# Attention decode with a mixer MLP: the last K transpose moved up in a block, and the wo products laid out as two wide rows

## Chip, core and metric

The program runs on one core of a Trainium2 chip. Its time is the device time of one execution in microseconds; the median of several executions is compared.

## The reference

One token, x of width 1024, goes through two branches whose results are added to x. What is computed, cut to what matters:

```python
xn = layernorm(x)
# A: attention over a cache of 65,536 positions, 4 KV heads of 8 query heads each, 128 wide
q = (xn @ wq).reshape(32 heads, 128)
p = softmax(q . k_cache * 128 ** -0.5)        # k_cache, v_cache: [4, 65536, 128] bf16
o = p . v_cache
A = o.reshape(4096) @ wo                      # wo: [4096, 1024]
# B: a mixer and an MLP on the same xn
h  = gelu(layernorm(xn) @ w1); hs = shift(h) @ w2; x1 = xn + hs
B  = x1 + gelu(layernorm(x1) @ w3) @ w4       # w4: [3584, 1024]
out = x + A + B
```

With one position the shifts of the mixer leave nothing of h, so the product with w2 is taken with a vector of zeros. The two caches are 64 MB each; with the weights some 170 MB are read.

## The kernel before, in words

The program is raw engine code. Python helpers record each operation in the list of its engine (`_Q`), with the semaphore waits that its buffers (`_B`) call for, and the lists are emitted in that order: what stands earlier in the source is earlier on its engine. DMAs are issued by SP, in order, each after the waits of its own buffers, so a DMA that waits holds up those behind it.

SBUF has three slots of 64 KB per partition, KV[0] to KV[2]. The weights wq, w1, w2 and w3 use them first (lines 295 to 451: the query and the MLP's hidden vector gh_bf). Then the caches stream through in NBLK = 8 blocks of 32,768 positions, two for each KV head: K of a block takes slot 0 or 2 in turn, V always slot 1. Behind the last V, wo goes into slot 0, and w4 into slot 2 in four pieces of 17, 7, 3 and 1 rows (`w4_parts`).

A block has four sub-tiles n to n+3, and a softmax for each half, 2m and 2m+1. The functions that the loop at line 585 calls:

- `Ttr(n)` (L460), on DVE: transposes a sub-tile of K in place, as 32-bit words.
- `QK(n)` (L474), on TensorE: 16 products of 512 columns, four side by side in four column groups, into PSUM bank n % 4 of `S_ps`.
- `MAX(g)` (L481 to 484): the row maxima of two banks on DVE, and a small product that spreads them.
- `EXP(g)` (L491 to 502): the running bound on DVE, the exponential of two banks on ACT into `p_sb`.
- `PT(n)` (L505) and `PTr(n)` (L509): the probabilities turned by a product into the one bank `PT_ps`, and from there by a DVE transpose into half n % 2 of `pT_f`.
- `PV(n)` (L518): 16 products with V into `OT_ps`.
- `FLUSH(g)` (L529, L531): adds the half's result to `O_acc` on DVE.
- `combine(h)` (L535 to 550): at the end of a head, the normalised output into `o_bf`.
- `issue(i)`: the load of V of the next block, and then of K of the block after it. V's waits for the last PV of this block, since V has one slot.

TensorE's instructions of a head are one loop body, run four times; the other engines' are written out.

After the loop, `out_resid` and `out_rows` make the sum of x, xn, the mixer's part, wo and w4 in bank 0 of `S_ps`, as four rows of 256 columns at partitions 0, 32, 64 and 96. A product there has one column of weights and 256 moving columns. A last DVE copy (L637) and one DMA bring it out.

Of the kernel before, what the change touches and what calls it, by code (L numbers as in the profile page):

```python
# [8 lines left out]
ACTF = mybir.ActivationFunctionType  # L9
# [107 lines left out]
def _op(q, fn, reads=(), writes=(), partial=False, loop=False):  # L117
    _deps(q, reads, writes)
    ev = q.op(fn, True, loop)
    _done(ev, reads, writes, partial)  # L120
    return ev


def _grp(q, fns, reads=(), writes=(), partial=False):
    _deps(q, reads, writes)
    ev = None
    for i, fn in enumerate(fns):
        ev = q.op(fn, i == len(fns) - 1)
    _done(ev, reads, writes, partial)
    return ev  # L130
# [16 lines left out]
def bass_parallel_sum__gqa_block_cached__mixer_s_mlp__decode_kernel(  # L147
# [14 lines left out]
    D = A_x.shape[2]  # L162
# [5 lines left out]
    KT_D = D // P  # L168
# [10 lines left out]
    with ExitStack() as es:  # L179
# [195 lines left out]
        fns = []  # L375
# [80 lines left out]
        def Ttr(n):  # L456
            m, sub = divmod(n, 4)
            s = slot(3 + 2 * m)
            o = 4096 * sub
            _op(q_dve, lambda e: e.transpose(out=KV32[:, s, o:o + 4096], in_=KV32[:, s, o:o + 4096]), reads=[b_KV[s][sub]], writes=[b_KV[s][sub]], loop=True)  # L460
# [5 lines left out]
        def QK(n):  # L466
            m, sub = divmod(n, 4)
            s = slot(3 + 2 * m)
            fns = []
            for we in range(4):  # L470
                w_hi, e_ = divmod(we, 2)
                for cm in range(4):
                    mv = bass.AP(KV[:].tensor, s * SLOT + sub * 8192 + cm * 128 + w_hi * 64 + e_, [[kvstep, P], [512, 16], [2, 32]])
                    fns.append(lambda e, we=we, cm=cm, mv=mv: e.matmul(  # L474
                        S_ps[32 * cm:32 * cm + 32, n % 4, :], Ycur[:, we, :, :].rearrange("p a g -> p (a g)"), mv,
                        start=(we == 0), stop=(we == 3), tile_position=(0, 32 * cm)))
            _grp(q_pe, fns, reads=[b_KV[s][sub], b_Yc], writes=[b_S[n % 4]])

        def MAX(g):
            k = g % 2  # L480
            _op(q_dve, lambda e: e.reduce_max(mrow[:, k:k + 1], S_ps[:, 2 * k:2 * k + 2, :].rearrange("p b c -> p (b c)"), axis=AX.X), reads=b_S[2 * k:2 * k + 2], writes=[b_mrow[k]])  # L481
            _op(q_dve, lambda e: e.tensor_tensor(out=Rm[:, k, :], in0=sel16[:, :], in1=mrow[:, k:k + 1].broadcast_to([P, 16]), op=ALU.mult),  # L482
                reads=[b_mrow[k], b_const], writes=[b_R[k]], loop=True)
            _op(q_pe, lambda e: e.matmul(M_ps[:, 0:16], Lmat[:, :], Rm[:, k, :], start=True, stop=True),  # L484
                reads=[b_R[k], b_const], writes=[b_M])

        def EXP(g):
            k, o = g % 2, 1 - g % 2
            first = g % (2 * BPH) == 0
            if first:  # L490
                _op(q_dve, lambda e: e.tensor_reduce(out=brun[:, k:k + 1], in_=M_ps[:, 0:16], axis=AX.X, op=ALU.min), reads=[b_M], writes=[b_brun[k]])  # L491
            else:
                _op(q_dve, lambda e: e.tensor_reduce(out=Bst[:, k:k + 1], in_=M_ps[:, 0:16], axis=AX.X, op=ALU.min), reads=[b_M], writes=[b_B[k]])
                _op(q_dve, lambda e: e.tensor_tensor(out=brun[:, k:k + 1], in0=brun[:, o:o + 1], in1=Bst[:, k:k + 1], op=ALU.min),  # L494
                    reads=[b_brun[o], b_B[k]], writes=[b_brun[k]])
            _op(q_act, lambda e: e.activation(p_sb[:, :, :].rearrange("p b c -> p (b c)"), S_ps[:, 2 * k:2 * k + 2, :].rearrange("p b c -> p (b c)"), ACTF.Exp,  # L496
                                              bias=brun[:, k:k + 1], scale=SCALE, accum_out=lp[:, k:k + 1]),
                reads=b_S[2 * k:2 * k + 2] + [b_brun[k]], writes=b_p + [b_lp[k]], loop=True)
            if not first:
                _op(q_dve, lambda e: e.tensor_tensor(out=dd[:, k:k + 1], in0=brun[:, k:k + 1], in1=brun[:, o:o + 1], op=ALU.subtract),  # L500
                    reads=[b_brun[o], b_brun[k]], writes=[b_dd[k]])
                _op(q_act, lambda e: e.activation(ff[:, k:k + 1], dd[:, k:k + 1], ACTF.Exp), reads=[b_dd[k]], writes=[b_ff[k]])

        def PT(n):
            _op(q_pe, lambda e: e.matmul(PT_ps[:, :], permR[:, :], p_sb[:, n % 2, :], start=True, stop=True),  # L505
                reads=[b_p[n % 2], b_const], writes=[b_PT])

        def PTr(n):
            _op(q_dve, lambda e: e.transpose(out=pT_f[:, n % 2, :], in_=PT_ps[:, :]), reads=[b_PT], writes=[b_pT[n % 2]], loop=True)  # L509

        def PV(n):
            m, sub = divmod(n, 4)
            s = slot(4 + 2 * m)
            g, last = divmod(n, 2)
            fns = []
            for q in range(16):
                q4 = q % 4
                fns.append(lambda e, q=q, q4=q4: e.matmul(OT_ps[32 * q4:32 * q4 + 32, g % 2, :], pT_bf[:, n % 2, q, :, 1],  # L518
                                                          KV[:, s, 8192 * sub + 512 * q:8192 * sub + 512 * (q + 1)],
                                                          start=(last == 0 and q < 4), stop=(last == 1 and q >= 12), tile_position=(0, 32 * q4)))  # L520
            _grp(q_pe, fns, reads=[b_pT[n % 2], b_KV[s][sub]], writes=[b_OT[g % 2]], partial=(last == 1))
# [40 lines left out]
        def out_rows(items, reads, last=False):  # L562
            fns = []
            for lhs, rhs in items:
                for jj in range(4):
                    fns.append(lambda e, lhs=lhs, rhs=rhs, jj=jj: e.matmul(  # L566
                        S_ps[32 * jj:32 * jj + 1, 0, 0:256], lhs, rhs[:, 256 * jj:256 * jj + 256],
                        start=False, stop=last, tile_position=(0, 32 * jj), skip_group_check=True))
            _grp(q_pe, fns, reads=reads, writes=[b_OUT], partial=True)

        def out_resid():
            fns = []
            for j in range(KT_D):
                for jj in range(4):
                    fns.append(lambda e, j=j, jj=jj: e.matmul(
                        S_ps[32 * jj:32 * jj + 1, 0, j:256:8], acc[:, j:j + 1], ident_f[:, 32 * jj:32 * jj + 32],
                        start=(j == 0), stop=False, tile_position=(0, 32 * jj), skip_group_check=True))
            _grp(q_pe, fns, reads=[b_acc, b_const], writes=[b_OUT])

        def loop_sync(h):  # L580
            if h > 0:
# [3 lines left out]
        for m in range(NBLK):  # L585
            n = 4 * m
            h, nb = divmod(m, BPH)
            if nb == 0:
                loop_sync(h)
                q_pe.mark({q.loop_sem: q.count[q.loop_sem] for q in (q_dve, q_act)})  # L590
                YC(h)
            Ttr(n)
            QK(n)
            Ttr(n + 1)
            QK(n + 1)
            Ttr(n + 2)
            MAX(2 * m)
            EXP(2 * m)
            QK(n + 2)
            PT(n)  # L600
            PTr(n)
            PT(n + 1)
            PTr(n + 1)
            Ttr(n + 3)
            PV(n)
            QK(n + 3)
            if m == NBLK - 1:
                for i in range(len(w4_parts)):
                    for bk in b_KV[2]:
                        for sv, vv in list(bk.r.items()) + list(bk.w.items()):  # L610
                            b_W4[i].add_read((sv, vv))
                    w4_dma(i)
            PV(n + 1)
            MAX(2 * m + 1)
            EXP(2 * m + 1)
            FLUSH(2 * m)
            PT(n + 2)
            PTr(n + 2)
            PT(n + 3)
            PTr(n + 3)  # L620
            PV(n + 2)
            PV(n + 3)
            FLUSH(2 * m + 1)
            issue(6 + 2 * m)
            if m == NBLK - 2:
                kv_load(0, "wo", A_wo.rearrange("(p r) n -> p (r n)", p=P), SLOT)
            else:
                issue(7 + 2 * m)
            if nb == BPH - 1:
                combine(h)  # L630
        loop_sync(HKV)
        q_pe.mark({q.loop_sem: q.count[q.loop_sem] for q in (q_dve, q_act)})
        out_resid()
        out_rows([(o_bf[:, j:j + 1], KV[:, 0, j * D:(j + 1) * D]) for j in range(32)], b_KV[0] + [b_o])
        for i, (r0, nr) in enumerate(w4_parts):
            out_rows([(gh_bf[:, r:r + 1], KV[:, 2, r * D:(r + 1) * D]) for r in range(r0, r0 + nr)], [b_W4[i], b_gh], last=(i == len(w4_parts) - 1))
        _op(q_dve, lambda e: e.tensor_copy(orow[:, :], OUT), reads=[b_OUT], writes=[b_orow])  # L637
# [82 lines left out]
```

## Time and profile before

| | us |
|---|---|
| median of 9 executions | 403.44 (401.97 to 405.21) |
| the profiled execution, time | 402.67 |
| its span, first to last instruction | 401.3 |
| busy: DVE, PE, ACT, POOL | 223.0, 183.4, 23.3, 7.1 |
| the 16 DMA engines' share of the span, queue q1 | 98.5% |
| mean granted TensorE clock | 0.608 |

The span is what the profile covers; the time of the same execution is 1.37 us more. In the views, L12 is line 12 of the kernel; PE is a TensorE product and PEld the load of its weights; a wait is given with the instruction that ended it. The chain of waits is followed back from the last instruction. Timeline lines give start and length in us. A line of the table of windows gives a stretch of the span, its length, the busy time of PE, PEld, DVE, ACT and POOL with the number of instructions, the granted TensorE clock, the busy share of the DMA engines and what they moved in GB/s. The share can exceed 1 a little in a short stretch, as a packet is counted where it begins.

### The profile page before, as it was taken

To read this page: it belongs to the slowest core of one execution; us is meant where nothing else is said; L and a number is where in the kernel's file an instruction comes from. 1 tells how busy PE (TensorE), PEld (TensorE's weight loads), DVE (VectorE), ACT (ScalarE), POOL (GpSimd) and SP (SyncE) were. 2 spreads that over 40 slices of the span, in tenths; PEclk is the share of its full clock that TensorE was granted. 3 is DMA by queue.
4 is the path that set the end of the run, shared out by engine and by line. 5 is a ranking of instruction groups with operands and counts; after the bars stand their busy time and mean duration, and the time that the engine had idled before them with its cause. 6 is when DMAs were issued, how large, how long until landed. Compare 5 with 4: busy or idle time off the path is not lost.

```text
span 401.3 us, 3672 instructions
## 1 busy us (share of the span) xinstructions
PE 183.4 (46%) x1627; PEld 65.9 (16%) x1627; DVE 223.0 (56%) x259; ACT 23.3 (6%) x49; POOL 7.1 (2%) x30
## 2 busy tenths in 40 slices
PE   0044767254335553561357235614551464245625
PEld 0022435011101120120012101101120111001323
DVE  0024221966397549645964795467748772976300
ACT  1000000011001100110011000101010101011000
POOL 5000000000000000000000000000000000000000
PEclk9997666556655555566557655555585555555776
DMA  9999999999999999999999999999999999999995
GB/s 418 418 394 482 394 491 425 420 418 431 400 431 425 470 400 438 431 444 405 438 425 425 425 444 451 438 419 431 431 418 444 438 438 438 425 418 425 418 416 208
DMA packets 3760, 169.99 MB, mean 424 GB/s; under 512 B 548, under 2 KB 552, under 8 KB 808
## 3 DMA queue, kind: packets, MB, share of 16 engines
q1 hardware_dynamic: 3608, 169.87, 98.5%
q8 instruction: 6, 0.10, 0.1%
q10 hardware_dynamic: 144, 0.00, 0.0%
q14 instruction: 2, 0.02, 0.0%
HBM read 169.87 MB, written 0.00 MB: 423 GB/s over the span
## 4 chain that ended last, share of the span: by engine, by line
DMA 55%; DVE 25%; PE 17%; issue 1%; ACT 1%; SPq 1%; POOL 0%
DMA KV<-in_A_k_cache_dram 42%; DVE KV L460 17%; DMA KV<-in_B_w_dram 8%; DMA KV<-in_A_x_dram 5%; PE S_ps L474 4%; PE OT_ps L518 3%; PE S_ps L411 3%; DVE pT_f L509 2%; PE M_ps L426 2%; PE PT_ps L505 2%; PE S_ps L379 1%; DVE mrow L481 1%; ACT p_sb L496 1%; DVE Yall L395 1%; DVE pT_f L419 1%
## 5 line engine op out<-in xcount | busy, mean ns | idle before, releaser
L460 DVE STREAM_TRANSPOSE KV<-KV 128x4096 f32<-128x4096 f32 x32 | 140.0, 4412 | 14.5 <-DMA KV<-in_A_k_cache_dram 14.5
L474 PE MATMUL S_ps<-KV,Ycur 128*32 128x512 bf16 x512 | 60.7, 623 | 97.5 <-DVE KV L460 97.5
L518 PE MATMUL OT_ps<-KV,pT_f 128*32 128x512 bf16 x512 | 57.4, 613 | 7.2 <-DMA KV<-in_A_v_cache_dram 7.2
L509 DVE STREAM_TRANSPOSE pT_f<-PT_ps 128x512 f32<-128x512 f32 x32 | 23.0, 717 | 34.1 <-PE PT_ps L505 34.1
L474 PEld LDWEIGHTS S_ps<-KV,Ycur 128*32 128x32 bf16 x512 | 14.3, 126 | 133.9 <-DVE KV L460 116.3
L496 ACT ACTIVATE p_sb<-S_ps,brun 128x1024 bf16<-128x1024 f32 x16 | 17.8, 1114 | 280.4 <-DVE brun L494 189.8
L505 PE MATMUL PT_ps<-p_sb,permR 128*128 128x512 bf16 x32 | 18.1, 567 | 26.6 <-ACT p_sb L496 13.6
L481 DVE TENSOR_REDUCE mrow<-S_ps 128x1 f32<-128x1024 f32 x16 | 19.3, 1205 | 16.0 <-PE S_ps L474 16.0
L518 PEld LDWEIGHTS OT_ps<-KV,pT_f 128*32 128x32 bf16 x512 | 17.4, 137 | 39.4 <-issue 27.4
L529 DVE SCALAR_TENSOR_TENSOR O_acc<-O_acc,ff,OT_ps 128x512 f32<-128x512 f32 x12 | 8.9, 745 | 21.9 <-PE OT_ps L518 21.9
L484 PE MATMUL M_ps<-Rm,Lmat 128*128 128x16 bf16 x16 | 3.1, 193 | 30.3 <-DVE Rm L482 30.2
L411 PE MATMUL S_ps<-KV 128*32 128x512 bf16 x88 | 12.6, 565 | 2.7 <-DVE KV L359 2.7
L339 DVE CAST KV<-KV 128x8 f32<-128x8 bf16 x1 | 0.2, 172 | 22.1 <-DMA KV<-in_A_x_dram 22.1
L637 DVE CAST orow<-S_ps 128x256 bf16<-128x256 f32 x1 | 0.4, 425 | 18.8 <-PE S_ps L566 18.8
L505 PEld LDWEIGHTS PT_ps<-p_sb,permR 128*128 128x128 bf16 x32 | 3.3, 102 | 41.2 <-ACT p_sb L496 21.0
L566 PE MATMUL S_ps<-KV,gh_bf 128*1 128x256 bf16 x112 | 6.0, 381 | 8.9 <-DMA KV<-in_B_w_dram 8.9
L426 PE MATMUL M_ps<-ident_f,pT_f 64*128 64x2 f32 (+2 forms) x32 | 7.9, 373 | 2.4 <-DVE pT_f L419 2.4
L484 PEld LDWEIGHTS M_ps<-Rm,Lmat 128*128 128x128 bf16 x16 | 1.6, 103 | 43.8 <-DVE Rm L482 43.8
L426 PEld LDWEIGHTS M_ps<-ident_f,pT_f 64*128 64x128 f32 (+2 forms) x32 | 7.7, 326 | 4.7 <-DVE pT_f L419 3.3
L419 DVE COPY pT_f<-S_ps 64x512 f32<-64x512 f32 (+1 forms) x3 | 2.1, 686 | 11.3 <-PE S_ps L411 11.3
L364 PE MATMUL M_ps<-KV 8*128 8x8 bf16 x1 | 0.2, 184 | 15.9 <-DVE Dmat_f L363 15.9
L379 PE MATMUL S_ps<-KV 128*32 128x512 bf16 x64 | 6.0, 556 | 1.4 <-DVE KV L359 1.4
(83 smaller groups left out, 86.8 us busy)
## 6 DMA issues: line engine op xcount, KB each, us to landing
KV<-in_B_w_dram SPq DMA_DIRECT2D x1, 7168.0 KB, 48.0
KV<-in_B_w_dram SPq DMA_DIRECT2D x1, 4352.0 KB, 24.7
KV<-in_B_w_dram SPq DMA_DIRECT2D x2, 2048.0 KB, 28.1
KV<-in_B_w_dram SPq DMA_DIRECT2D x1, 1792.0 KB, 28.6
KV<-in_B_w_dram SPq DMA_DIRECT2D x1, 768.0 KB, 30.0
KV<-in_B_w_dram SPq DMA_DIRECT2D x1, 256.0 KB, 30.2
KV<-in_A_k_cache_dram SPq DMA_DIRECT2D x8, 42.9
KV<-in_A_v_cache_dram SPq DMA_DIRECT2D x8, 24.0
```

Source lines behind the costliest of these rows:

```text
L379: fns.append(lambda e, j=j, b=b, jj=jj: e.matmul(S_ps[32 * jj:32 * jj + 32, b, :], xn_bf[:, j:j + 1].broadcast_to([P, 32]), KV[:, 0, j * H ...
L411: fns.append(lambda e, j=j, k=k, mv=mv: e.matmul(S_ps[32 * (k % 4):32 * (k % 4) + 32, bank + k // 4, :], vec[:, j:j + 1].broadcast_to([P, ...
L419: _op(q_dve, lambda e, b=b, nb=nb: e.tensor_copy(pT_f[0:32 * nb, b, :], S_ps[0:32 * nb, bank + b, :]), reads=[b_S[bank + b]], writes=[b_pT ...
L426: fns.append(lambda e, b=b, nb=nb, c=c: e.matmul(M_ps[:, c0 + 16 * b + c:c0 + 16 * b + 4 * nb:4], pT_f[0:32 * nb, b, c:512:4], ident_f[0:3 ...
L460: _op(q_dve, lambda e: e.transpose(out=KV32[:, s, o:o + 4096], in_=KV32[:, s, o:o + 4096]), reads=[b_KV[s][sub]], writes=[b_KV[s][sub]], l ...
L474: fns.append(lambda e, we=we, cm=cm, mv=mv: e.matmul(S_ps[32 * cm:32 * cm + 32, n % 4, :], Ycur[:, we, :, :].rearrange("p a g -> p (a g)") ...
L481: _op(q_dve, lambda e: e.reduce_max(mrow[:, k:k + 1], S_ps[:, 2 * k:2 * k + 2, :].rearrange("p b c -> p (b c)"), axis=AX.X), reads=b_S[2 * ...
L496: _op(q_act, lambda e: e.activation(p_sb[:, :, :].rearrange("p b c -> p (b c)"), S_ps[:, 2 * k:2 * k + 2, :].rearrange("p b c -> p (b c)") ...
L505: _op(q_pe, lambda e: e.matmul(PT_ps[:, :], permR[:, :], p_sb[:, n % 2, :], start=True, stop=True), reads=[b_p[n % 2], b_const], writes=[b ...
L509: _op(q_dve, lambda e: e.transpose(out=pT_f[:, n % 2, :], in_=PT_ps[:, :]), reads=[b_PT], writes=[b_pT[n % 2]], loop=True)
L518: fns.append(lambda e, q=q, q4=q4: e.matmul(OT_ps[32 * q4:32 * q4 + 32, g % 2, :], pT_bf[:, n % 2, q, :, 1], KV[:, s, 8192 * sub + 512 * q ...
L529: _op(q_dve, lambda e: e.scalar_tensor_tensor(out=O_acc[:, 0:512], in0=O_acc[:, 0:512], scalar=ff[:, k:k + 1], in1=OT_ps[:, k, :], op0=ALU ...
```

## The change

In the loop, `Ttr(n + 3)` comes right after the first half's `EXP`, ahead of `PT(n)`; `QK(n + 3)` follows `PTr(n)`. The second half's `MAX` and `EXP` come before `PV(n)`, and `PV(n)`, `PV(n + 1)` and `FLUSH(2m)` are woven among the second half's `PT`. In the last block the w4 loads stand behind `QK(n + 3)`, as before.

In the tail, the residual and wo are summed in bank 1 as two rows of 512 columns at partitions 0 and 32: 16 products in place of 32, and 64 in place of 128. One row is then copied by DVE, the other by ACT, into half 0 of `pT_f`, whose first 64 partitions POOL has set to zero; four fp32 products with columns of the identity carry the quarters of the two rows to the four rows of bank 0, on which the w4 products add as before.

```diff
--- before.py
+++ after.py
@@ -568,14 +568,23 @@
                         start=False, stop=last, tile_position=(0, 32 * jj), skip_group_check=True))
             _grp(q_pe, fns, reads=reads, writes=[b_OUT], partial=True)
 
-        def out_resid():
-            fns = []
-            for j in range(KT_D):
-                for jj in range(4):
-                    fns.append(lambda e, j=j, jj=jj: e.matmul(
-                        S_ps[32 * jj:32 * jj + 1, 0, j:256:8], acc[:, j:j + 1], ident_f[:, 32 * jj:32 * jj + 32],
-                        start=(j == 0), stop=False, tile_position=(0, 32 * jj), skip_group_check=True))
-            _grp(q_pe, fns, reads=[b_acc, b_const], writes=[b_OUT])
+        def resid_rows():
+            _grp(q_pe, [lambda e, j=j, jj=jj: e.matmul(
+                S_ps[32 * jj:32 * jj + 1, 1, j:512:8], acc[:, j:j + 1], ident_f[:, 64 * jj:64 * jj + 64],
+                start=(j == 0), stop=False, tile_position=(0, 32 * jj), skip_group_check=True) for j in range(KT_D) for jj in range(2)],
+                reads=[b_acc, b_const], writes=[b_S[1]])
+
+        def wo_rows():
+            _grp(q_pe, [lambda e, j=j, jj=jj: e.matmul(
+                S_ps[32 * jj:32 * jj + 1, 1, :], o_bf[:, j:j + 1], KV[:, 0, j * D + 512 * jj:j * D + 512 * (jj + 1)],
+                start=False, stop=(j == 31), tile_position=(0, 32 * jj), skip_group_check=True) for j in range(32) for jj in range(2)],
+                reads=b_KV[0] + [b_o], writes=[b_S[1]], partial=True)
+            _op(q_dve, lambda e: e.tensor_copy(pT_f[0:1, 0, :], S_ps[0:1, 1, :]), reads=[b_S[1]], writes=[b_pT[0]])
+            _op(q_act, lambda e: e.activation(pT_f[32:33, 0, :], S_ps[32:33, 1, :], ACTF.Copy), reads=[b_S[1], b_pT[0]], writes=[b_pT[1]])
+            _grp(q_pe, [lambda e, jj=jj: e.matmul(
+                S_ps[32 * jj:32 * jj + 1, 0, 0:256], ident_f[0:64, 32 * (jj // 2):32 * (jj // 2) + 1], pT_f[0:64, 0, 256 * (jj % 2):256 * (jj % 2) + 256],
+                start=True, stop=False, tile_position=(0, 32 * jj), skip_group_check=True) for jj in range(4)],
+                reads=[b_pT[0], b_pT[1], b_const], writes=[b_OUT])
 
         def loop_sync(h):
             if h > 0:
@@ -596,13 +605,10 @@
             Ttr(n + 2)
             MAX(2 * m)
             EXP(2 * m)
+            Ttr(n + 3)
             QK(n + 2)
             PT(n)
             PTr(n)
-            PT(n + 1)
-            PTr(n + 1)
-            Ttr(n + 3)
-            PV(n)
             QK(n + 3)
             if m == NBLK - 1:
                 for i in range(len(w4_parts)):
@@ -610,12 +616,15 @@
                         for sv, vv in list(bk.r.items()) + list(bk.w.items()):
                             b_W4[i].add_read((sv, vv))
                     w4_dma(i)
-            PV(n + 1)
+            PT(n + 1)
             MAX(2 * m + 1)
+            PTr(n + 1)
             EXP(2 * m + 1)
-            FLUSH(2 * m)
+            PV(n)
             PT(n + 2)
             PTr(n + 2)
+            PV(n + 1)
+            FLUSH(2 * m)
             PT(n + 3)
             PTr(n + 3)
             PV(n + 2)
@@ -630,8 +639,9 @@
                 combine(h)
         loop_sync(HKV)
         q_pe.mark({q.loop_sem: q.count[q.loop_sem] for q in (q_dve, q_act)})
-        out_resid()
-        out_rows([(o_bf[:, j:j + 1], KV[:, 0, j * D:(j + 1) * D]) for j in range(32)], b_KV[0] + [b_o])
+        _op(q_pool, lambda e: e.memset(pT_f[0:64, 0, :], 0.0), writes=[b_pT[0]])
+        resid_rows()
+        wo_rows()
         for i, (r0, nr) in enumerate(w4_parts):
             out_rows([(gh_bf[:, r:r + 1], KV[:, 2, r * D:(r + 1) * D]) for r in range(r0, r0 + nr)], [b_W4[i], b_gh], last=(i == len(w4_parts) - 1))
         _op(q_dve, lambda e: e.tensor_copy(orow[:, :], OUT), reads=[b_OUT], writes=[b_orow])
```

## Prediction

> **What bounds the kernel now.** I read the page's busy table, slices and DMA queues first, then the chain of waits, then the timeline of one block and of the tail, and last the table of windows at the end.
>
> ```profile
> PE 183.4 (46%) x1627; PEld 65.9 (16%) x1627; DVE 223.0 (56%) x259; ACT 23.3 (6%) x49; POOL 7.1 (2%) x30
> ...
> DMA  9999999999999999999999999999999999999995
> ...
> q1 hardware_dynamic: 3608, 169.87, 98.5%
> ...
> HBM read 169.87 MB, written 0.00 MB: 423 GB/s over the span
> ```
>
> No compute engine is busy for more than 56% of the span, while the 16 DMA engines are busy for 98.5% of it, moving 169.87 MB. All the idleness of the transfers is 1.5% of 401.3 us, 6.0 us. The next view, windows of the span's end, says where most of that lies.
>
> ```profile
> 395.00:396.00 1.00, 0.81 (x16) 0.23 (x8) 0.00 (x0) 0.00 (x0) 0.00 (x0) 0.50 0.93 361
> 396.00:397.00 1.00, 0.66 (x16) 0.43 (x20) 0.00 (x0) 0.00 (x0) 0.00 (x0) 0.50 0.41 158
> 397.00:398.00 1.00, 0.73 (x20) 0.29 (x12) 0.00 (x0) 0.00 (x0) 0.00 (x0) 0.84 0.06 23
> 398.00:399.00 1.00, 0.65 (x16) 0.28 (x16) 0.00 (x0) 0.00 (x0) 0.00 (x0) 1.00 0.02 8
> 399.00:401.30 2.30, 0.13 (x4) 0.00 (x0) 0.42 (x1) 0.00 (x0) 0.00 (x0) 0.88 0.00 1
> ```
>
> The last two columns are the DMA share and GB/s. From 396 on the idle share is 0.59 + 0.94 + 0.98 + 2.30 = 4.8 us of the 6.0; the rest is the start (first packets about 1 us in) and crumbs. From 44 to 104 us and from 104 to 380 us the windows give a share of 1.00. So the loop that the change reorders leaves no transfer time to win, save under 0.5 us. Second reading: between 397 and 398 the share is 0.06, one engine of 16. A single late engine decides when the last w4 piece is complete.
>
> The timeline of the end of block 4, the start of block 5 and the tail:
>
> ```profile
> 259.88 0.33 SPq L290 DMA_DIRECT2D KV<-in_A_v_cache_dram  x1
> ...
> 263.96 13.10 DVE L460 STREAM_TRANSPOSE KV<-KV 128x4096 f32<-128x4096 f32 x3 [3.13 <-DMA KV<-in_A_k_cache_dram]
> ...
> 380.60 3.67 PE L566 MATMUL S_ps<-KV,o_bf 128*1 128x256 bf16 x128 [0.62 <-DMA KV<-in_A_wo_dram]
> ...
> 392.01 3.80 PE L566 MATMUL S_ps<-KV,gh_bf 128*1 128x256 bf16 x68 [7.75 <-DMA KV<-in_B_w_dram]
> ...
> 396.34 1.39 PE L566 MATMUL S_ps<-KV,gh_bf 128*1 128x256 bf16 x28 [0.53 <-DMA KV<-in_B_w_dram]
> ...
> 398.85 0.28 PE L566 MATMUL S_ps<-KV,gh_bf 128*1 128x256 bf16 x4 [0.15 <-DMA KV<-in_B_w_dram]
> ```
>
> V of block 5 is issued at 259.88, 4.1 us before K of block 5 has landed (263.96): the queue is refilled before it is dry. In the tail every group of products waits for its transfer; TensorE stands idle for 7.75 us ahead of w4.
>
> [...] the queue "q8 instruction" has 6 packets and 0.10 MB, 16 KB each. [...] the DMA view of 385 to 388 us shows one, with 2.2% of 16 engines' 3 us = 1.06 us. [...] Here the granted clock is 0.50 in most of the loop, 1.00 from 378 to 386 and 0.50 again at 388.
>
> **The change, part by part**, against the profiled execution's own 402.67 us (span 401.3, 1.37 around it), which lies 0.77 under the median of 403.44.
>
> *Loop order.* The same instructions run in another order; no DMA is added. Times from the first transpose of block 5 (263.96). Now: three transposes to 13.1, softmax of the first half to 15.3, PT/PTr twice to 19.2, fourth transpose to 23.5 (4.40), QK to 25.5 (1.90), second softmax, last PV ends at 33.8; SP issues V at 297.79. Then: the fourth transpose follows the softmax's small operations at 15.3 and ends at 19.7; QK(n+3) 19.7 to 21.6; its MAX (1.23 + 0.18), the M_ps product and the two small DVE operations, with PTr(n+1) between, to 24.2. PTr(n) waits behind the transpose on DVE, so PV(n) starts not when V lands (19.7) but at about 23.3. EXP to PT takes 1.26, so PT(n+2) at 25.5; PV(n+1) 26.1 to 28.0; PT(n+3), PV(n+2), PV(n+3) at half clock end at about 32.2. The block ends 1.6 us sooner, V and the next K are issued 5.7 us ahead of need in place of 4.1. **Worth 0**: they join a queue that still has work. Bounds: -0.5 (all crumbs of idleness) and 0; it turns into a loss only when the issue comes over 4 us later than now. The w4 issues move with QK(n+3) from 367.3 to 363.4, both long before wo has landed (380.6): 0.
>
> *Residual.* 32 two-pass fp32 products (64 records, 0.94 us) become 16 of twice the width: equal at most, done before wo lands, since the block's end moved forward too: 0.
>
> *wo.* Before, 128 products of 256 columns, four side by side, took 3.67 us at full clock: 32 rounds of 0.115. After, 64 of 512 columns, only two side by side: 32 rounds of 0.23, **7.3 us**, if the clock is full; at half clock the loads of L474's rounds start 0.427 apart: 13.7 us. Then DVE copies one row (nearest: L419, 0.69), ACT the other, waiting for DVE (L421, 0.59), and four fp32 products of 256 columns carry them. L543's 8 passes of 128 columns took 0.95 in a row; so between 0.5, four side by side, and 2.0, one after the other: I take 1.0. Handovers 0.2. Sum after wo: 7.3 + 2.5 = 9.8, from 380.6 to 390.4. w4's first piece lands at 392.0: hidden with 1.6 us to spare, **0**. Behind the carry on TensorE's queue stand all w4 products, and the output behind them, so this cover matters: w4's first three pieces take 3.80 + 1.39 + 0.50 = 5.7 us at half clock and must be done by 398.85. They may start at 393.1 at the latest, or at about 395.7 at full clock. The memset on POOL waits for PV(n+2) of the last block; nothing stands behind it there, and the DVE copy needs it only at 388: 0 (nearest L318, 0.52 us for 128x512 bf16).
>
> *Instructions.* The tail has 304 products and as many loads, 608 instructions; after, (32 + 64 + 8 + 112) x 2 = 432. By counting the instructions before each fetch (some 256 apart, at 43.7, 79.2, 106.2 and 145.1 us), I estimate the boundaries at about 235 and 491 into the tail, in step with the fetches seen at 386.1 and 395.9. The first stopped one engine for 1.06 us amid w4, and by the trace's packet records it was the engine that finished last: its share of w4's first piece came 1.2 us after the next engine's, and so it stayed to the end. After, the boundary of 491 is never reached; that of 235 falls some 27 instructions into w4 (208 come before), so its fetch moves later, to about 390 to 395, and may take another engine, or one that is done. Bounds 0 and -1.2. Nothing shows which engine a fetch takes; I take **-0.5**.
>
> Sum: 0 + 0 + 0 - 0.5 us. Added to the median: **402.9**. The end itself (one row of w4, 0.42 of DVE, the output's DMA) is unchanged.
>
> **Rivals.** (A, likeliest, 0.49) The transfers set the end and nothing moves by more than a measurement of this kernel can tell, about 0.3% (1.2 us): 402.3 to 404.5. For it: the share of 1.00 for 336 us. (B, 0.33) The late engine is freed: the fetch no longer delays the last w4 piece (-1.2), and earlier V issues remove up to 0.5: 403.44 - 1.2 to 1.7, 401.7 to 402.2, say 402.0. For it: one engine alone for 1.2 us. Against: one fetch is still to come in w4, and only this execution is known to have had it on the last engine. (C, 0.18) The two rows are too slow: TensorE runs the wo rounds at half clock, or the two groups don't go side by side, which alone makes 64 x 0.213 = 13.7 us. Then w4 starts at 380.6 + 13.7 + 3.5 (the carry doubled too) = 397.8 and the last piece waits for 5.7 us of older products: up to 4.6 us later, 408. It decides when the carry ends after 393.1 at half clock. Half a clock for the first 6.8 us only gives 391.1 + 2.5 = 393.6 at full clock afterwards and costs nothing. Against: the clock was full when wo ran[...]. Middle of C: 405.5. The change failing its purpose in the loop (V issued later) is in C with 0.03.
>
> **How the numbers follow.** A's own range is 402.3 to 404.5; with most of B and the near end of C the range is 401.3 to 404.9. Faster by over 0.3% is B, slower by over 0.3% is C.
>
> **What would show it.** Right: V issued about 1.6 us sooner after a block's first transpose (32.2, not 33.8), DMA share 1.00 in the loop, wo products some 7 us long, TensorE idle again ahead of w4's first piece, one instruction fetch fewer, and the last w4 products still waiting for a transfer. Wrong: w4's first products start on a wait for ACT or DVE, or blocks that start sooner (K landing less than 38.8 us apart).

## Result and profile after

The changed kernel takes 400.45 us (median of 10 executions, 400.20 to 400.85), against 403.59 for the kernel before (31 executions, 401.93 to 405.21): a ratio of 0.9925, 95% interval 0.991 to 0.994. It is 0.75% faster, 3.1 us: more than the forecast of 402.9, and below its range (401.3 to 404.9). The spread shrank as well, from 3.3 us to 0.65.

First the page of the changed kernel: the DMA slices, the queues q1 and q8 (packets, MB, share of 16 engines), what HBM gave, and the group of the K transposes (busy us, mean ns, then the idle time ahead of them).

```profile
DMA  9999899999999999999999999999999999999995
...
q1 hardware_dynamic: 3608, 169.87, 98.6%
q8 instruction: 5, 0.08, 0.1%
...
HBM read 169.87 MB, written 0.00 MB: 425 GB/s over the span
...
L460 DVE STREAM_TRANSPOSE KV<-KV 128x4096 f32<-128x4096 f32 x32 | 140.3, 4421 | 44.2 <-DMA KV<-in_A_k_cache_dram 44.2
```

The same bytes cross in a shorter span: 425 GB/s where it was 423. The busy share, 98.6% and 98.5%, hardly tells the two apart. One line does speak: DVE now stands idle for 44.2 us ahead of its K transposes, waiting for K, where the page of before has 14.5:

```profile
L460 DVE STREAM_TRANSPOSE KV<-KV 128x4096 f32<-128x4096 f32 x32 | 140.0, 4412 | 14.5 <-DMA KV<-in_A_k_cache_dram 14.5
```

The compute of a block is over sooner, so V of the next block is issued sooner. Fetches of instructions fell from six to five, as forecast.

The timeline of the changed kernel, at the places shown of before (start and length in us):

```profile
254.04 0.33 SPq L290 DMA_DIRECT2D KV<-in_A_v_cache_dram  x1
...
263.62 13.10 DVE L460 STREAM_TRANSPOSE KV<-KV 128x4096 f32<-128x4096 f32 x3 [8.62 <-DMA KV<-in_A_k_cache_dram]
...
379.90 8.76 PE L578 MATMUL S_ps<-KV,o_bf 128*1 128x512 bf16 x64 [2.63 <-DMA KV<-in_A_wo_dram]
...
390.59 2.03 PE L566 MATMUL S_ps<-KV,gh_bf 128*1 128x256 bf16 x68
394.45 0.94 PE L566 MATMUL S_ps<-KV,gh_bf 128*1 128x256 bf16 x28 [1.84 <-DMA KV<-in_B_w_dram]
...
396.96 0.28 PE L566 MATMUL S_ps<-KV,gh_bf 128*1 128x256 bf16 x4 [0.15 <-DMA KV<-in_B_w_dram]
```

V of block 5 is issued 9.6 us ahead of the complete landing of K of block 5; before it was 4.1. wo is complete at 379.8 where it was 380.5, and the last w4 products start at 396.96 where they started at 398.85. These 1.9 us are less than the medians' 3.1, as the profiled execution of before was a good one (402.67 against a median of 403.59); no slower one was profiled. At the landing of wo 0.7 of the 1.9 had been gained, counted to the last of the 16 engines, and 1.5 counted to their mean.

Now the question is why a queue that was never empty gained time. The window from 104 to 344 us of the kernel before (last three columns: granted TensorE clock, DMA share, GB/s):

```profile
104.00:344.00 240.00, 107.63 (x842) 31.46 (x834) 159.76 (x147) 15.29 (x33) 0.00 (x0) 0.55 1.00 429
```

and of the changed kernel:

```profile
104.00:344.00 240.00, 97.84 (x834) 27.29 (x834) 157.84 (x145) 15.27 (x33) 0.00 (x0) 0.58 1.00 432
```

Both have a busy share of 1.00, but 429 and 432 GB/s: 0.7% of 240 us is 1.7 us. A packet that takes longer is counted as busy all the while. In the trace's packet records a 64 KB packet takes 2.42 us; in the kernel before, 56 of them after 60 us took over 2.47, most of them 1 to 5 us after a V issue. After the issue at 182.02, five that began between 184.0 and 184.5 took 2.76, 4.08, 2.89, 4.04 and 4.16 us. The changed kernel has 5 such packets, and four of them follow an instruction fetch.

These packets account for the loss. What they took beyond 2.42 us, added up and divided by the 16 engines, is 1.65 us in before and 0.15 in the changed kernel: 1.50 more, while wo lands 1.53 us later by the mean of its 16 landings.

### The profile page after: what moved, and what is told of

It is laid out like the page before. It is cut to its first block, busy times and chain, and to the rows that moved or that the text cites. A ratio compares the mean times of both kernels' runs of the same rounds, so it can differ in the third digit from the quotient of the medians.

```text
span 399.4 us, 3500 instructions
## 1 busy us (share of the span) xinstructions
PE 177.4 (44%) x1539; PEld 61.9 (15%) x1539; DVE 221.3 (55%) x260; ACT 23.9 (6%) x50; POOL 7.6 (2%) x31
## 3 DMA queue, kind: packets, MB, share of 16 engines
q1 hardware_dynamic: 3608, 169.87, 98.6%
## 4 chain that ended last, share of the span: by engine, by line
DMA 58%; DVE 25%; PE 13%; issue 1%; ACT 1%; SPq 1%; POOL 0%
DMA KV<-in_A_k_cache_dram 45%; DVE KV L460 17%; DMA KV<-in_B_w_dram 8%; DMA KV<-in_A_x_dram 6%; PE S_ps L411 3%; PE OT_ps L518 2%; DVE mrow L481 2%; PE M_ps L426 2%; PE S_ps L474 2%; PE S_ps L379 2%; ACT p_sb L496 1%; DVE Yall L395 1%; DVE pT_f L509 1%; PE PT_ps L505 1%; DVE pT_f L419 1%
## 5 line engine op out<-in xcount | busy, mean ns | idle before, releaser
L460 DVE STREAM_TRANSPOSE KV<-KV 128x4096 f32<-128x4096 f32 x32 | 140.3, 4421 | 44.2 <-DMA KV<-in_A_k_cache_dram 44.2
L518 PE MATMUL OT_ps<-KV,pT_f 128*32 128x512 bf16 x512 | 46.6, 504 | 1.2 <-DVE pT_f L509 1.2
L474 PEld LDWEIGHTS S_ps<-KV,Ycur 128*32 128x32 bf16 x512 | 14.3, 126 | 159.8 <-DVE KV L460 142.3
L529 DVE SCALAR_TENSOR_TENSOR O_acc<-O_acc,ff,OT_ps 128x512 f32<-128x512 f32 x12 | 9.0, 747 | 14.5 <-PE OT_ps L518 14.5
L518 PEld LDWEIGHTS OT_ps<-KV,pT_f 128*32 128x32 bf16 x512 | 12.9, 114 | 23.8 <-issue 15.7
L578 PE MATMUL S_ps<-KV,o_bf 128*1 128x512 bf16 x64 | 8.8, 443 | 2.6 <-DMA KV<-in_A_wo_dram 2.6
```

Source lines behind the costliest of these rows:

```text
L474: fns.append(lambda e, we=we, cm=cm, mv=mv: e.matmul(S_ps[32 * cm:32 * cm + 32, n % 4, :], Ycur[:, we, :, :].rearrange("p a g -> p (a g)") ...
L529: _op(q_dve, lambda e: e.scalar_tensor_tensor(out=O_acc[:, 0:512], in0=O_acc[:, 0:512], scalar=ff[:, k:k + 1], in1=OT_ps[:, k, :], op0=ALU ...
L578: _grp(q_pe, [lambda e, j=j, jj=jj: e.matmul(S_ps[32 * jj:32 * jj + 1, 1, :], o_bf[:, j:j + 1], KV[:, 0, j * D + 512 * jj:j * D + 512 * (j ...
```

## Experiments

Two theories were put to the test. **L, the lead**: V's issue came too late for those DMA engines that are done with K early. The 16 engines complete a K some 2 us apart, so a lead of 4 us over the last engine is only some 2 over the first. **F, the fetch**: the gain came from the tail, where an instruction fetch had stopped the last engine for 1.06 us. Leads below are those of V of blocks 1 to 7 in the profiled execution: V's issue in the timeline of SP, against the landings of K's 16 parts in the trace.

**e1, the loop's new order with the old tail.** The functions `resid_rows` and `wo_rows`, their calls and the memset were replaced by `out_resid` and `out_rows` of before.

> The new loop order with the old tail (residual and wo as four rows of 256). Theory L (the lead of V's issue): in the kernel before, V is issued 4.0 to 5.2 us ahead of the landing of the K in flight, too late for the DMA engines that finish early, and packets of 64 KB stretch there from 2.42 us to as much as 4.16; after, it is issued 8.0 to 9.6 us ahead. L expects most of the 3.1 us here: 400.4 to 401.4 us, V issued 8 us or more ahead, stretched packets gone. Theory F (the tail's instruction fetch that stopped the last engine for 1.06 us): this kernel still fetches at about 384, so it stays at 403 or at best 402.5.

Measured: 400.47 us, ratio 0.9911 (0.9885 to 0.9937), the whole gain. The lead is 6.0 to 7.4 us over the first engine. The page counts six fetches, as before:

```profile
q8 instruction: 6, 0.10, 0.1%
```

By the packet records the fifth ran at 385.0 us for 1.07 us, just where it had cost time. But here it met one of the engines that were 1.7 us or more ahead of the last one (wo's parts landed from 377.3 to 377.7 on eleven engines, at 379.5 on the last), and the last was not moved. F falls: beside the loop's order, the tail's change adds nothing that these runs show.

**e2, the tail alone**, put into the kernel before.

> The old loop order with the new tail (two rows of 512, carried by four products). L: the leads of V stay at 4 to 5 us, so 402.4 to 403.6 us, at most the 1.2 us of the late engine gained. F: 400.5 to 402.0, most of the gain. If the two rows cost time by themselves, over 404.

Measured: 402.96 us, ratio 0.9985 (0.9968 to 1.0002), not told apart from no change. F's 400.5 to 402.0 did not come out; the interval still leaves room for up to 1.3 us, so in the old order the fetch may cost something. The leads stay at 1.9 to 3.2 us over the first engine, and 103 packets are stretched.

**e3, only the transpose moved:**

```diff
             EXP(2 * m)
+            Ttr(n + 3)
             QK(n + 2)
...
             PTr(n + 1)
-            Ttr(n + 3)
             PV(n)
```

> The kernel before with only the fourth transpose moved ahead of PT(n); MAX and EXP of the second half stay behind both first PVs, the tail is the old one. By the durations of before a block ends some 0.5 us sooner, so the lead grows to 4.5 to 5.7 us. L: 402.4 to 403.4 us, between before and the new loop, nearer to before. Rival: the transpose's place is all there is to the loop's gain, as QK(n+3) starts 4 us sooner: 400.4 to 401.4, like the whole loop.

Measured: 400.47 us, ratio 0.9913 (0.9887 to 0.9939). The rival's number came out, yet not for its reason: the leads grew more than I had estimated, to 3.2 to 6.1 us over the first engine, and 4 packets are stretched. In the timeline of this kernel V is issued at

```profile
179.18 0.33 SPq L290 DMA_DIRECT2D KV<-in_A_v_cache_dram  x1
```

and K is there for DVE at

```profile
185.68 4.45 DVE L460 STREAM_TRANSPOSE KV<-KV 128x4096 f32<-128x4096 f32 x1 [5.54 <-DMA KV<-in_A_k_cache_dram]
```

6.5 us later, in place of 4.4 before:

```profile
182.02 0.33 SPq L290 DMA_DIRECT2D KV<-in_A_v_cache_dram  x1
...
186.45 4.45 DVE L460 STREAM_TRANSPOSE KV<-KV 128x4096 f32<-128x4096 f32 x1 [3.47 <-DMA KV<-in_A_k_cache_dram]
```

**e12, only the weaving**: `Ttr(n + 3)` of the changed kernel put back behind `PTr(n)`.

> The changed kernel with the fourth transpose back behind PTr(n), so only the weaving of the second half's MAX and EXP and the first PVs is left of the loop's change. By the changed kernel's durations the transpose ends some 2.5 us later and so does the block: V issued 32.9 us after a block's first transpose in place of 30.4, the lead 3.3 to 4.5 us over the first engine. L: still enough, 400.3 to 401.0 us. If it is the transpose's place itself that counts: 402.5 to 404.

Measured: 400.55 us, ratio 0.9923 (0.9895 to 0.9951), but in two groups: six executions at 400.2 to 400.6, two at 403.0. The profiled one is of the second group (403.05): its lead over the first engine is 2.0 to 2.9 us in five of seven issues, less than the 3.3 to 4.5 expected, and 82 packets are stretched. The leads of the other seven were not recorded. So this order stands on the edge; either half of the loop's change can give the gain, and with the transpose (e3) all six executions had it. This profile also shows which engine to measure to: at block 3 its lead was 6.3 us over the last engine but 2.0 over the first, and 27 packets were stretched, while in e5 below 5.6 to 7.0 us over the last, with 3.5 or more over the first, cost next to nothing.

**e4, e9, e5, e6: the lead taken away again.** The changed kernel, with SP held back before each V issue by k copies on ACT that follow the block's last PV (`p_flat` is `p_sb` as 1024 columns; a copy takes 1.06 us):

```diff
+        def slow_issue(k, m):
+            if m < NBLK - 1:
+                for _ in range(k):
+                    _op(q_act, lambda e: e.activation(p_flat, p_flat, ACTF.Copy), reads=[b_OT[1]], writes=b_p)
+                _deps(q_sp, [b_p[0]], [])
...
             FLUSH(2 * m + 1)
+            slow_issue(k, m)
             issue(6 + 2 * m)
```

Four copies (e4):

> The changed kernel, with each block's V issue (and the K or wo load behind it) held back on SP by four copies of p_sb onto itself on ACT that start after the block's last PV, some 4.4 us; ACT has nothing else to do then. Nothing else changes. L: the lead falls back to 3.6 to 5.2 us and the time to 402.4 to 404 us, the stretched packets are back. F, or a gain from a faster compute chain: 400.3 to 400.9, as the queue still has 4 us of work when V is issued.

Measured: 403.38 us, ratio 0.9991 (0.9967 to 1.0015): the whole gain is gone, and the executions spread again from 401.2 to 405.6. The window of e4 shows the busy share of 1.00 with the old rate:

```profile
104.00:344.00 240.00, 98.38 (x834) 27.12 (x834) 156.31 (x145) 41.04 (x58) 0.00 (x0) 0.59 1.00 429
```

Three copies (e9):

> The same with three copies, some 3.15 us: the lead is about 3.0 us over the first engine, 5.2 over the last, at the edge. L: 400.4 to 401.6 us. The proportional rival: 402.3 to 403.

Measured: 400.62 us, 0.9924 (0.9899 to 0.9949). Six executions took 400.4 to 400.7, two 401.5 and 402.4: the edge.

Two copies (e5):

> The changed kernel with each V issue held back by two copies on ACT, some 2.1 us (four cost 2.9 us of time). The lead over the first DMA engine to land K becomes about 4.0 us, over the last about 6.3. L: still clear of the 3.0 us (first engine) up to which packets were seen stretched, so 400.3 to 400.8 us. A rival in which every microsecond of lead counts in proportion (2.9 us lost for 4.2 us): 401.5 to 402.2.

Measured: 400.47 us, 0.9926 (0.9898 to 0.9953). The median loses nothing; one of six executions took 401.44.

Six copies (e6):

> The same with six copies, some 6.3 us: the lead falls to some 0 to 1 us over the first engine and 2 over the last[...]. L: each block now loses the whole shortfall, damped by half as a late K also starts the next block late: 1.0 to 1.7 us for each of seven blocks, 406 to 412 us, with idle DMA engines at every V issue. The proportional rival: 404.5 to 405.2.

Measured: 408.83 us, 1.0131 (1.0093 to 1.0169). Now the engines do stand idle, and even the busy share falls:

```profile
104.00:344.00 240.00, 96.75 (x834) 27.09 (x834) 154.94 (x144) 56.15 (x72) 0.00 (x0) 0.59 0.98 420
```

So the loss is not in proportion to the lead: next to nothing in the median down to some 3 us over the first engine (e5, e9), 2.8 us of time for the next copy of 1.06 us (e4), and 5.5 for the two after it (e6).

**e10, the control**: six copies, but behind V's issue, so that only the K behind it is late.

```diff
             issue(6 + 2 * m)
+            slow_issue(6, m)
```

> Control for e6: the same six copies on ACT, but SP waits for them after V's issue, so only the K (or wo) load behind V is issued 6.3 us later. K has V's 19 us of transfer ahead of it. L: 400.3 to 400.9 us, though ACT does the same extra work. If the copies themselves, or any late issue, cost the time of e6: 406 or more.

Measured: 400.59 us, 0.9925 (0.9902 to 0.9948). The copies cost nothing; what counts is when the queue gets its next load, not when it gets the one after.

**e7, the lead without the change.** The kernel before, with V in two loads:

```diff
             PV(n + 1)
+            if m < NBLK - 1:
+                v_load(v_src(m + 1), 0)      # sub-tiles 0 and 1
...
             FLUSH(2 * m + 1)
-            issue(6 + 2 * m)
+            if m < NBLK - 1:
+                v_load(v_src(m + 1), 1)      # sub-tiles 2 and 3
```

> The kernel before, its compute untouched, with V loaded in two halves of 4 MB, each with its own semaphore: the half with sub-tiles 0 and 1 is issued as soon as PV(n+1) is done, some 6.6 us ahead of the other, which is issued where V was. So the queue is refilled some 10 us ahead without any change of the order of work. L: 400.3 to 401.0 us, the whole gain without the change. If the gain came from the order of the work on DVE or TensorE itself, or from the smaller number of stalls in a block: 403 to 404.

Measured: 401.16 us, 0.9933 (0.9907 to 0.9959), a little outside L's range. The compute is as slow as before, and most of the gain is there. The missing 0.7 us would fit the smaller packets, which was not tested alone: V comes in 32 KB packets, twice as many, and by the landings a block's 16 MB take 38.8 us where the changed kernel takes 38.7.

**e8, both**: the changed kernel with V in two loads.

> The changed kernel with V loaded in two halves, as in e7. The lead grows from some 6 us over the first engine to about 10 or more. L: beyond some 3 us more lead buys nothing, and e7's two packets in place of one cost it 0.08 us a block, so 400.8 to 401.3 us, slower than the changed kernel. If lead still counts: under 400.2.

Measured: 401.16 us, 0.9940 (0.9917 to 0.9963), as L expected and the same as e7. Lead beyond the need buys nothing.

**e11, fewer bytes.**

```diff
-        _dma(q_sp, chan("w2"), lambda e: e.dma_start(out=KV[:, 1, 8 * D:16 * D], in_=rows_src(B_w2, 0, 8)), writes=b_w2)
...
-        proj(1, 8 * D, D, g_bf, 3, b_w2 + [b_const], 272)
-        _op(q_dve, lambda e: e.tensor_tensor(out=x1, in0=xn, in1=M_ps[:, 272:272 + KT_D], op=ALU.add), reads=[b_xn, b_M], writes=[b_x1])
-        _op(q_dve, lambda e: e.tensor_tensor(out=acc[:], in0=acc[:], in1=M_ps[:, 272:272 + KT_D], op=ALU.add), reads=[b_acc, b_M], writes=[b_acc])
+        _op(q_dve, lambda e: e.tensor_copy(x1, xn), reads=[b_xn], writes=[b_x1])
```

> The changed kernel without the load of w2 and its product, whose other factor is a vector of zeros (with one position the shifts leave nothing of h); the two additions of that zero go too. 2.10 MB less to move. If bytes set the end, at 433 GB/s (the rate between 180 and 190 us of the changed kernel) 4.84 us less: 395.3 to 396.0 us. If the end is set by the chains of work after the transfers: less than 2 us gained.

Measured: 395.58 us, 0.9801 (0.9776 to 0.9826) against the kernel before: 4.87 us less than the changed kernel's 400.45 (the kernel before took 403.94 beside this run and 403.59 beside that one), where 4.84 was worked out from bytes alone. It is faster than both kernels, as the product it leaves out is one with zeros. With the lead in place, bytes set the time of this kernel.

All leads in one table, in us. The leads and the stretched packets (64 KB, over 2.47 us, after 60 us) are those of the profiled execution, whose time stands beside the median; "extra" is what the stretched packets took beyond 2.42 us, per engine. In e7 and e8 only K's packets are counted, as V's are of 32 KB.

| kernel | over first engine | over last engine | stretched | extra | profiled | median |
|---|---|---|---|---|---|---|
| e6, six copies | -0.7 to 2.8 | 1.3 to 5.0 | 100 | 3.05 | 407.35 | 408.83 |
| e4, four copies | 1.4 to 2.9 | 3.6 to 5.6 | 108 | 1.99 | 402.59 | 403.38 |
| before | 1.8 to 3.1 | 4.0 to 5.2 | 56 | 1.65 | 402.67 | 403.59 |
| e2, tail only | 1.9 to 3.2 | 3.8 to 4.9 | 103 | 1.74 | 402.19 | 402.96 |
| e12, weaving only | 2.0 to 4.4 | 4.1 to 8.4 | 82 | 2.05 | 403.05 | 400.55 |
| e9, three copies | 2.1 to 3.9 | 4.1 to 5.8 | 40 | 1.09 | 401.48 | 400.62 |
| e3, transpose only | 3.2 to 6.1 | 5.2 to 8.1 | 4 | 0.14 | 400.30 | 400.47 |
| e5, two copies | 3.5 to 4.8 | 5.6 to 7.0 | 8 | 0.22 | 400.43 | 400.47 |
| changed | 5.8 to 7.1 | 7.9 to 9.6 | 5 | 0.15 | 400.67 | 400.45 |
| e11, no w2 | 5.7 to 7.2 | 8.0 to 9.5 | 4 | 0.12 | 395.52 | 395.58 |
| e1, loop only | 6.0 to 7.4 | 8.1 to 9.4 | 10 | 0.17 | 400.38 | 400.47 |
| e10, K late | 6.0 to 6.8 | 8.1 to 9.0 | 5 | 0.16 | 400.59 | 400.59 |
| e7, V in halves, on before | 7.9 to 9.6 | 9.8 to 12.0 | 0 | 0.00 | 401.40 | 401.16 |
| e8, V in halves, on the changed kernel | 9.4 to 10.0 | 11.1 to 11.8 | 24 | 0.20 | 401.11 | 401.16 |

The extra time and the loss go together: against the changed kernel, wo lands later by 1.53 us (before), 1.43 (e2), 1.81 (e4), 0.83 (e9) and 1.90 (e12), each by the mean of its 16 landings, and the extra time is larger by 1.50, 1.60, 1.84, 0.95 and 1.91. In e6 it explains 2.9 of 6.4 us; there the engines also stood idle. Taken issue by issue over the kernels with V in one load, leads of 1 to 2 us over the first engine cost 0.5 us each in the mean (6 issues; extra time per engine in the 12 us behind the issue), leads of 2.0 to 2.6 cost 0.3 (16 issues), and those of 3.3 us or more 0.02 (46 issues, none over 0.09).

## Why the prediction was wrong

- **The step that failed** is "Worth 0: they join a queue that still has work", with its bound of -0.5 and the sentence that it "turns into a loss only when the issue comes over 4 us later than now". The runs put the loop's order at -3.1 us (e1). Two readings led there. The share of 1.00 was taken as proof that no transfer time was lost, while stretched packets fill a share as well as good ones; the rate would have told: in before it is 433 GB/s from 44 to 104 us and 429 from 104 to 380. And the lead of 4.1 us was measured to the moment at which DVE could start, the landing of the *last* of 16 engines; the first was done 1.8 to 3.1 us after V's issue, which is less than is needed. The forecast's own sign of being wrong came: K lands 38.77 us apart in the mean, where it was 38.91.
- **The direction of the risk** was read the wrong way round. The forecast saw a later issue as the danger and an earlier one as worthless. In fact the kernel before stood past the edge: taking 2.1 us of lead from the changed kernel costs nothing (e5), taking 4.2 costs 2.9 (e4).
- **The block's end** was forecast at 32.2 us after the first transpose; it is 30.4 (263.62 to 294.00). The chain of the steps was right up to PT(n+3), at 27.6 where 28.0 was worked out. The last two PVs were costed at half clock; they ran largely at full clock (granted 0.96 from 291.76 to 294.00), 32 products in 2.19 us where the same block had taken 3.25 before (granted 0.56 from 294.50 to 297.75), and others 3.6. It made the lead over the last engine larger than forecast, 7.9 to 9.6 us and not 5.7. This part of the lead was not foreseen, and not needed either: e3 and e5, with less of it, gain as much.
- **The fetch** was put at -0.5. It shows as 0 in the presence of the lead: e1 fetches as before and is as fast as the changed kernel. That one execution of before lost 1.2 us to it was read rightly: there the last landing of w4's first piece came 11.5 us after the last of wo (380.5 to 392.0), in e1 10.3 (379.5 to 389.8). So this one pair of profiles owes 1.2 of its 1.9 us at the end to the fetch, and looks as if F were true; six executions of e1 say otherwise. In the changed kernel the fetch in w4 moved to 393.9 us, as forecast. The landings of the changed kernel show what the fetches of 16 KB do: of the 16 parts of a K, two come over 1 us behind the first at 67.5 us, four at 106 and five at 145, one more for each of the fetches at 79.3, 103.3 and 142.3, and five still at wo. Each met another engine and made it late by some 1.5 us, side by side and not one on top of the other. This is most of the 2 us between the first engine and the last.
- **The tail** was right in substance. From wo's first product to the last carry product it takes 10.8 us (379.90 to 390.66) where 9.8 was worked out: wo's rounds took 8.76 in place of 7.3, an estimate for a full clock: from 380.8 to 383.8 the granted clock was 0.50 and their loads start 0.43 apart, from 384.2 to 388.6 it was 1.00; the copies took 0.68 and 0.59, the carry 0.61. The cover was thinner than said: w4's first piece is complete at 390.1, so its products started 0.5 us late. They caught up, and TensorE waits 1.84 us again ahead of the second piece. The edge at 395.7 stayed far away.
- **The rivals.** B had the sign, for the wrong reason: its "up to 0.5" for earlier V issues was the term that carried everything, and its 1.2 for the engine does not show beside it (e1). A, the likeliest, held that nothing would move; C did not occur.

## What to carry to other kernels

In a kernel bound by transfers, look at the rate in GB/s stretch by stretch, not at the busy share (here 429 and 432 GB/s under the same share of 1.00), and measure the lead of each refill to the *first* DMA engine that runs out, not to the landing of the whole. Here some 3 us of it were enough; below that most loads lost time, above it nothing more was won, and both means that were tried gave it: another order of work, or a buffer freed in halves. Once the lead was there, fewer bytes were what still helped.

## What the runs showed of the hardware

The need of some 3 us: V's loads joined without loss where every lead over the first engine was 3.2 us or more (e3, e5), and with stretched packets at 1.4 to 2.9 (e4). Near this edge executions of one kernel differ from each other by up to 2.8 us (e12). All of this is for packets of 64 KB; whether smaller ones need less was not tested.

What happens in these 3 us is not shown by these runs. The first packets of all in before, at 1 us into the span on engines that had been idle, are stretched too, to between 2.5 and 3.4 us; whether both have one reason was not tested.

The packet of an instruction fetch of 16 KB took 1.02 to 1.09 us in the changed kernel (0.89 to 1.12 over all runs), where a data packet of 64 KB takes 2.42. In the changed kernel four of the five stretched packets begin where a fetch ends (three of 16 KB, and one of 8 KB in queue q14 that took 0.33 us), and take 0.5 to 0.7 us over 2.42. For the fetches of 16 KB, the two together are the 1.5 us by which the landings show an engine late after a fetch of 16 KB.
